# Attention and two feed-forward layers on one core: remaining queries' scores as 64x64 products, and the work around them moved between steps

## The chip, the cores and the metric

One core of one Trainium2 chip runs the kernel. The metric is device time in microseconds (us); lower is better. Three runs of the kernel before gave a median of 1094.99 us (1094.66 to 1095.34).

## The reference

Inputs are float32. Attention has 4 batches of 8 heads, 576 positions, 64 wide; each feed-forward layer (FFN) takes 2304 tokens of 512 through 2048 hidden values.

```python
q_rot, k_rot = (rotate(q), rotate(k))
scores = scale * np.matmul(q_rot, k_rot.transpose(0, 1, 3, 2))
scores = scores - np.max(scores, axis=-1, keepdims=True)
attn = np.exp(scores)
attn = attn / (np.sum(attn, axis=-1, keepdims=True) + 1e-09)
x = np.matmul(attn, v)                                # attention
h = x @ w_in;  x = (h - np.tanh(h)) @ w_out           # first FFN
h = x @ w_in;  x = (h * (1.0 / (1.0 + np.exp(-h)))) @ w_out   # second FFN, other weights
```

## The kernel before

Attention (`attention`, L336) goes through 16 pairs of heads, `i` = 0 to 15. The 576 positions of a head are 4 blocks of 128 (`NJ` = 4, `MAIN` = 512) and 64 remaining ones (`REM`). A pair has nine score tiles: for each of the four query blocks one tile for head 0 and one for head 1 (128 queries by 576 keys), and a ninth with the remaining 64 queries of both heads.

A pair is worked off in five **steps**, `z` = 0 to 4. Steps 0 to 3 each compute the two score tiles of one query block, step 4 the ninth tile. A step issues, in this order:

- `scores` (L501) on PE into two PSUM buffers `sc` that all tiles share in turn. Head 0 sits in rows 0 to 63 of the array and head 1 in rows 64 to 127; each tile is two products of 288 keys. A float32 product shows as two records in the trace, so a step has eight. The ninth tile multiplies all 128 rows by a block-diagonal copy `qr` of the remaining queries (L510).
- transposes on PE: `qk_turn` (L428) turns rotated q and k of the **next** pair into `kq`, one half of the partitions at a time (for halves 0 and 1 in the steps that `QK_K` = (4, 0) names; for pair 0 `QK_0`); `p_turn` (L564) turns the previous step's probabilities `p` with 64x64 transposes for the two halves of partitions in turn; `full_block` (L700) has 128x128 transposes: `rest_turn` (L592, the last 128 columns of two `p` tiles, in steps 3 and 4), `spread` (L541, the reciprocal sums) and `rem_turn` (L440, remaining positions of the next pair).
- `row_max` (L515) on DVE, `exps` (L520) on ACT, and copies of the transposes out of PSUM. `early` copies come before the exponentials on ACT, `outs` after them. `ON_DVE` names the (`u`, half) copies of `p_turn(u)` that DVE does; ACT does the others.
- one or more small pieces (`conv.run`, L753) of the conversion of FFN weights, on DVE and ACT.
- `pv` (L600) on PE: 20 products of `v` with the previous pair's turned probabilities, `PV_N` = (6, 4, 6, 4, 0) of them per step. They run in twos, one for each half of the output partitions of one PSUM tile `x`.

The rotations of pair `i + 2` run on POOL. Transposes go into three PSUM buffers `tp` in turn, `p` has three SBUF buffers. Each engine takes its instructions in the order written here; nothing else sets it. In the last pair (`i` = 15) `on_scores_near` (L1188) splits the first FFN block `xin` into a high part `xh` (ACT) and a low part `xl` (DVE), and after step 4 the first FFN product (`gemm_h`, L814) starts. In pair 0 the stretches without work on PE have dummy transposes (`warm`, L484).

```python
            if h < 2:
                r, c0 = half[h], REM - h * REM
                l = kq[r, 1, REM + j * 128:REM + (j + 1) * 128]
            else:
                r, c0, l = slice(0, 128), REM, qr2[i % 2]
            if i == NP - 1 and z:
                on_scores_near(z)
```

Of the kernel before, what the change touches and what calls it, by code (L numbers as in the profile page):

```python
# [8 lines left out]
F32 = mybir.dt.float32  # L9
# [4 lines left out]
ACTF = mybir.ActivationFunctionType  # L14
# [15 lines left out]
def kernel(  # L30
# [14 lines left out]
    B, H, S, D = q.shape  # L45
# [5 lines left out]
    NJ = S // 128  # L51
# [274 lines left out]
    NPV = 4 * (NJ + 1)  # L326
    Q0 = 256
    WARM = (5, 5, 6, 2, 4, 1, 6)
    WARM_Z = (0, 7, 7, 5, 3)
    ON_DVE = ((1, 1), (2, 1), (4, 0), (4, 1))  # L330
    QK_K, QK_0 = (4, 0), (4, 3)
    R_K = 1
    PV_N = (6, 4, 6, 4, 0)
    CONV_K = (0, 1, 1, 1, 1)

    def attention(conv, on_rope_done, on_scores_near, on_scores_done):  # L336
# [10 lines left out]
        csq = rp.tile([128, 2, NJ, D], F32, name="csq")  # L347
        csr = rp.tile([128, 2, D], F32, name="csr")
        vr2 = [ap.tile([128, 2, D], F32, name=f"vr{i}") for i in range(2)]
        qr2 = [qkp[i].tile([128, 128], F32, name=f"qr{i}") for i in range(2)]  # L350
        raw_t, rot_t, v_t, qk_t = {}, {}, {}, {}
        half = (slice(0, 64), slice(64, 128))

# [87 lines left out]
            PE.transpose(tp, rot_t[i][2].rearrange("p h d -> p (h d)"), ident)  # L441

        def rem_evict(i, tp):
            for r in half:
                ACT.activation(out=qr2[i % 2][r, r], in_=tp[r, 0:64], func=ACTF.Copy)
            ACT.activation(out=qk_t[i][:, 0].rearrange("p (a c) -> p a c", c=REM)[:, ::S // REM],
                           in_=tp[:, 64:128].unsqueeze(1).to_broadcast([128, 2, REM]), func=ACTF.Copy)

# [10 lines left out]
        def q_rope(j0, j1):  # L459
            xm, xr = raw_t[0]  # L460
            if j0 == 0:
                rot_t[0][1] = rp.tile([128, NJ, 2, D], F32, tag="aq", name="aq", bufs=2)
            js = slice(j0, j1)
            sh = [128, 2, j1 - j0, D]
            o = rot_t[0][1][:, js].rearrange("p j h d -> p h j d")
            x = xm[1].rearrange("p h (j d) -> p h j d", j=NJ)[:, :, js]
            b = ap.tile([128, 2, S], F32, tag="p", name="p", bufs=3)[:, :, 0:(j1 - j0) * D]
            b = b.rearrange("p h (j d) -> p h j d", d=D)
            hd = D // 2
            DVE.tensor_tensor(out=o, in0=x, in1=csq[:, 0, js].unsqueeze(1).to_broadcast(sh), op=ALU.mult)  # L470
# [30 lines left out]
        def scores(g):  # L501
            i, n = divmod(g, NTI)
            h, j = tiles[n]
            kq = qk_t[i]
            sc = score_tile(g)
            if h < 2:
                r, c0 = half[h], REM - h * REM
                l = kq[r, 1, REM + j * 128:REM + (j + 1) * 128]
            else:
                r, c0, l = slice(0, 128), REM, qr2[i % 2]  # L510
            for e in range(2):
                PE.matmul(sc[:, e, 0:HALF], lhsT=l, rhs=kq[r, 0, c0 + e * HALF:c0 + (e + 1) * HALF],  # L512
                          start=True, stop=True)
# [6 lines left out]
        def exps(g):  # L520
            i, n = divmod(g, NTI)
            if n == 0:
                sum_t[i] = ap.tile([128, NTI], F32, tag="sums", name="sums", bufs=2)
            sc, st = s_t.pop(g), st_t.pop(g)
            h, u = tiles[n]
            if h != 1:
                p_t[i, u] = ap.tile([128, 2, S], F32, tag="p", name="p", bufs=3)
            p = p_t[i, u][:, h % 2]
            ACT.activation(out=p.rearrange("p (e s) -> p e s", e=2), in_=sc[:, :, 0:HALF],  # L529
                           func=ACTF.Exp, bias=st, accum_out=sum_t[i][:, n:n + 1])  # L530
# [33 lines left out]
        def p_turn(i, u):  # L564
# [10 lines left out]
                cols = [p0 + c * 128 for c in range(NJ) for p0 in (0, S + REM)]  # L575
            else:
                cols = [c * 128 for c in range(NJ)] + [S - 128]
            for x, c in enumerate(cols):
                for w, r in enumerate(half):
                    PE.transpose(tp[w][:, x * 64:x * 64 + 64], p[r, c:c + 128], ident[r, r])  # L580

            def out(w):
                act = (u, w) not in ON_DVE
                if u < NJ:
                    evac(ptm[:, :, :, o + 64 * w:o + 64 * w + 64],
                         tp[w].rearrange("p (c h q) -> p c h q", c=NJ, h=2), act)
                else:
                    evac(ptm[:, :, w, o:o + 64], tp[w][:, 0:MAIN // 2].rearrange("p (c q) -> p c q", c=NJ), act)
                    evac(ptr[half[w], o:o + 64], tp[w][64:128, MAIN // 2:MAIN // 2 + 64], act)
            return [((u, w) not in ON_DVE, lambda w=w: out(w)) for w in range(2)]  # L590

        def rest_turn(i, e, t, act):  # L592
            for a in range(2):
                PE.transpose(t[:, a * 128:a * 128 + 128],  # L594
                             p_t[i, 2 * e + a].rearrange("p h s -> p (h s)")[:, MAIN:MAIN + 128], ident)
            return act, lambda: evac(pt_t[i][e][1][:, 0:Q0], t, act)

        x_t = {}

# [42 lines left out]
        nc.sync.dma_start(out=csk, in_=cs_main)  # L642
        nc.scalar.dma_start(out=csr, in_=cs_rem)
        load_qk(0)
        for t in (*vr2, *qr2):
            DVE.memset(t, 0.0)
        load_v(0)
        load_qk(1)
# [24 lines left out]
        i = z = 0  # L673
        while True:
            live, more = i < NP, i + 1 < NP
            qk_at = QK_K if i else QK_0
            n0 = i * NTI + 2 * z
            gs = range(n0, n0 + (2 if z < NJ else 1)) if live else ()
            if live:
# [20 lines left out]
            def full_block():  # L700
                if live:
                    es = ((), (1,), (), (0,), ())[z] if i else ()
                else:
                    es = (1, 0) if z == 1 else ()
                rest = live and z in (3, NJ)
                rem = more and z == (R_K if i else 3)
                if rest or rem or es:
                    tp = ps.tile([128, 512], F32, tag="tp", name="tpb", bufs=3)
                if rest:
                    (early if z == NJ else outs).append(rest_turn(i, z - 3, tp[:, Q0:], z == NJ))  # L710
# [31 lines left out]
            if live:  # L742
                for _ in range(4):
                    if rq:
                        rq.pop(0)[1]()
            for g in gs:
                exps(g)
            for act, f in outs:
# [515 lines left out]
```

## Time and profile before

| what | value |
|---|---|
| median of three runs | 1094.99 us |
| the profiled execution | 1093.34 us |
| its span, first to last instruction | 1091.6 us |
| PE busy | 1077.0 us (99%) |
| DVE busy | 826.0 us (76%) |
| ACT busy | 647.5 us (59%) |
| POOL busy | 239.2 us (22%) |

A busy PE in this table is a matmul in flight, and matmuls overlap: two half-array matmuls side by side count once, and a half array that waits beside one that works counts as busy. So 99% does not say that PE could not be faster; the start times in the timeline do. DMA moves 126 MB in 91276 packets, 36% of its engines' time.

### The profile page before, as it was taken

Reading aid. Unit: us, or ns where it says so; the run is one execution under the profiler, and the core shown is the slowest. Engines: PE = TensorE matmul, PEld = TensorE weight load, DVE = VectorE, ACT = ScalarE, POOL = GpSimd, SP = SyncE. Lnnn points to the kernel's source line nnn. Section 1 sums busy time; section 2 is a strip of 40 time slices with the busy share of each in tenths; the row PEclk is TensorE's granted clock in tenths of the full one; section 3 lists DMA queues with packets and bytes.
Section 4 is the critical chain, followed back from the end, with each engine's and each line's share of the span. In section 5 each row is a group of like instructions: output and inputs, shape, how many; then the busy total and the mean of one; then the engine's idle time right before and its main releaser. Section 6 shows DMA issues by size and latency. Waiting matters only on the chain.

```text
span 1091.6 us, 18837 instructions
## 1 busy us (share of the span) xinstructions
PE 1077.0 (99%) x6925; PEld 880.8 (81%) x6925; DVE 826.0 (76%) x1425; ACT 647.5 (59%) x1395; POOL 239.2 (22%) x311
## 2 busy tenths in 40 slices
PE   9899999999999999999999999999999999999998
PEld 7676767676678898888888898888888889999997
DVE  6777777777679967988999978987546356767775
ACT  6787877778666766667666666544334335333342
POOL 6776676864010200211001100310000000000000
PEclk9999999999999999999999999999999999999999
DMA  6232323332403530444465541665345112122042
GB/s 177 66 109 82 111 80 111 86 109 60 138 17 126 173 107 20 157 152 146 156 210 174 173 136 48 209 216 183 117 135 183 58 40 97 58 78 87 24 142 77
DMA packets 91276, 126.34 MB, mean 116 GB/s; under 512 B 16432, under 2 KB 57008, under 8 KB 91184
## 3 DMA queue, kind: packets, MB, share of 16 engines
q1 hardware_dynamic: 90592, 124.75, 36.0%
q8 instruction: 54, 0.88, 0.3%
q10 hardware_dynamic: 592, 0.39, 0.1%
q14 instruction: 38, 0.31, 0.1%
HBM read 88.93 MB, written 36.18 MB: 115 GB/s over the span
## 4 chain that ended last, share of the span: by engine, by line
PE 94%; POOL 2%; ACT 2%; DMA 1%; DVE 1%; issue 1%; SPq 0%; POOLq 0%; ACTq 0%; DVEq 0%
PE hp L827 36%; PE acc L904 27%; PE sc L512 9%; PE x L615 8%; PE M L988 7%; PE tpp L580 3%; PE tpq L435 1%; PE acc L1132 1%; PE tpb L545 1%; ACT kq L436 1%; PE tpb L594 1%; POOL bm L417 1%; ACT p L529 0%; DMA xm<-in_k_dram 0%; DMA csr<-rope_rem_dram 0%
## 5 line engine op out<-in xcount | busy, mean ns | idle before, releaser
L827 PE MATMUL hp<-xh,w 128*128 128x512 f32 (+1 forms) x1280 | 389.4, 370 | 0.5 <-ACT xh L808 0.5
L827 PEld LDWEIGHTS hp<-xh,w 128*128 128x128 f32 x1280 | 235.3, 189 | 42.4 <-issue 1.3
L827 PE MATMUL hp<-xl,w 128*128 128x512 f32 (+1 forms) x640 | 236.9, 370 | 0.2 <-DVE xl L809 0.2
L838 ACT ACTIVATE t<-hp 128x512 f32<-128x512 f32 (+1 forms) x120 | 66.8, 556 | 244.0 <-PE hp L827 241.4
L904 PE MATMUL acc<-gh,w 128*128 128x512 f32 (+1 forms) x640 | 193.9, 369 | 0.0
L872 DVE TENSOR_TENSOR gl<-t,gh 128x512 fp32r<-128x512 f32 (+1 forms) x120 | 77.0, 642 | 112.4 <-ACT gh L870 112.2
L517 DVE TENSOR_REDUCE st<-sc 128x1 f32<-128x576 f32 x144 | 104.5, 754 | 63.1 <-PE sc L512 48.4
L827 PEld LDWEIGHTS hp<-xl,w 128*128 128x128 f32 x640 | 121.1, 189 | 19.8 <-DVE xl L809 0.5
L529 ACT ACTIVATE p<-sc,st 128x576 f32<-128x576 f32 x144 | 105.4, 737 | 53.1 <-DVE st L517 45.6
L904 PEld LDWEIGHTS acc<-gh,w 128*128 128x128 f32 x640 | 117.3, 189 | 20.2 <-issue 0.3
L251 POOL TENSOR_TENSOR w<-wf,w 128x512 fp32r<-128x512 f32 x32 | 45.5, 1435 | 349.9 <-ACT w L250 345.1
L904 PE MATMUL acc<-gl,w 128*128 128x512 f32 (+1 forms) x320 | 117.9, 369 | 0.0
L512 PE MATMUL sc<-kq 64*128 64x288 f32 x512 | 100.3, 429 | 2.7 <-ACT p L529 0.6
L512 PEld LDWEIGHTS sc<-kq 64*128 64x128 f32 x512 | 63.3, 186 | 32.5 <-ACT p L529 20.9
L904 PE MATMUL acc<-w,gh 128*128 128x512 f32 x288 | 89.0, 390 | 0.0
L615 PE MATMUL x<-pt,vm 128*64 128x256 f32 (+1 forms) x512 | 75.8, 418 | 0.0
L870 ACT ACTIVATE gh<-t 128x512 fp32r<-128x512 f32 (+1 forms) x120 | 70.6, 588 | 6.2 <-PE acc L904 6.2
L988 PE MATMUL M<-w,gh 128*128 128x256 f32 x384 | 70.3, 283 | 0.0
L904 PEld LDWEIGHTS acc<-gl,w 128*128 128x128 f32 x320 | 60.4, 189 | 10.0
L580 PE MATMUL tpp<-ident,p 64*128 64x64 f32 x1184 | 65.4, 227 | 0.0
L988 PEld LDWEIGHTS M<-w,gh 128*128 128x128 f32 x384 | 61.9, 192 | 2.3
L580 PEld LDWEIGHTS tpp<-ident,p 64*128 64x128 f32 x1184 | 57.7, 140 | 7.4 <-ACT pt L557 2.9
(138 smaller groups left out, 1918.8 us busy)
## 6 DMA issues: line engine op xcount, KB each, us to landing
raw<-in_moe_w_in_dram SPq DMA_DIRECT2D x32, 512.0 KB, 4.1
raw<-in_moe_w_out_dram SPq DMA_DIRECT2D x28, 512.0 KB, 3.8
xin<-xd SPq DMA_DIRECT2D x56, 256.0 KB, 4.6
wd<-wa SPq DMA_DIRECT2D x48, 256.0 KB, 2.2
wf<-wd SPq DMA_DIRECT2D x48, 256.0 KB, 3.9
pd<-xo SPq DMA_DIRECT2D x34, 256.0 KB, 2.8
xo<-pd SPq DMA_DIRECT2D x18, 256.0 KB, 5.2
xm<-in_q_dram SPq DMA_DIRECT2D x16, 256.0 KB, 3.2
```

Source lines behind the costliest of these rows:

```text
L251: (DVE if key[0] == 3 else POOL).tensor_tensor(out=w[:, 1].rearrange("p (a b) -> p a b", a=a), in0=src, in1=w[:, 0].bitcast(F32).rearrange ...
L512: PE.matmul(sc[:, e, 0:HALF], lhsT=l, rhs=kq[r, 0, c0 + e * HALF:c0 + (e + 1) * HALF], start=True, stop=True)
L517: DVE.tensor_reduce(out=st, in_=s_t[g][:, :, 0:HALF], op=ALU.max, axis=AX.XY, negate=True)
L529: ACT.activation(out=p.rearrange("p (e s) -> p e s", e=2), in_=sc[:, :, 0:HALF], func=ACTF.Exp, bias=st, accum_out=sum_t[i][:, n:n + 1])
L580: PE.transpose(tp[w][:, x * 64:x * 64 + 64], p[r, c:c + 128], ident[r, r])
L615: PE.matmul(x[o, 0:w], lhsT=l, rhs=r, start=(cc == 0), stop=(cc == NJ))
L827: PE.matmul(hp, lhsT=w[:, a, ws], rhs=bb, start=(n == 0), stop=(n == 3 * KD - 1))
L838: ACT.activation(out=t, in_=hp, func=ACTF.Tanh, scale=0.5 if l else 1.0)
L870: ACT.activation(out=gh, in_=t, func=ACTF.Copy)
L872: DVE.tensor_tensor(out=gl, in0=t, in1=gh.bitcast(F32), op=ALU.subtract)
L904: PE.matmul(acc, lhsT=a, rhs=bb, start=(fi == 0 and n == 0), stop=(fi == NH - 1 and n == 2))
L988: PE.matmul(prod_t[name][:, tt], lhsT=al[i], rhs=bw[j], start=(first and tt == 0 and x == 0), stop=(last and tt == nt - 1 and x == 2))
```

## The change

- The ninth tile's scores become, for each of two key halves, two products of 64 queries by 288 keys: head 0 in rows 0 to 63 and partitions 0 to 63 of the output, head 1 in rows 64 to 127 and partitions 64 to 127. The remaining queries go into free columns of `kq`; `qr`, its two copies per pair and its two memsets are gone.
- `rest_turn` of step 4 goes. Those columns are turned by `p_turn` of the ninth tile in step 0 of the next pair, as four more 64-row transposes; each half copies its part (`out`). So two `p` tiles live longer, and `p` has four buffers.
- The first half of the ninth tile's copies goes from DVE to ACT (`ON_DVE`).
- `pv` gives 4, 4, 6, 4, 2 products in steps 0 to 4.
- In pair 1 the second `qk_turn` goes from step 0 to step 1 (`QK_AT`), and step 0 gets five dummy transposes (`WARM_Z`).
- In the last pair, steps 2 to 4 have no pieces of weight conversion, and the splits of `xin` go from steps 2, 3 and 4 (one, two, one) to steps 3 and 4 (two each), ahead of the exponentials.

```diff
-    WARM_Z = (0, 7, 7, 5, 3)
-    ON_DVE = ((1, 1), (2, 1), (4, 0), (4, 1))
-    QK_K, QK_0 = (4, 0), (4, 3)
+    WARM_Z = (0, 7, 7, 5, 3, 5)
+    ON_DVE = ((1, 1), (2, 1), (4, 1))
+    QK_AT = ((4, 3), (4, 1), (4, 0))
-    PV_N = (6, 4, 6, 4, 0)
+    PV_N = (4, 4, 6, 4, 2)
...
-            for r in half:
-                ACT.activation(out=qr2[i % 2][r, r], in_=tp[r, 0:64], func=ACTF.Copy)
+            ACT.activation(out=qk_t[i][:, 1, 0:REM], in_=tp[:, 0:64], func=ACTF.Copy)
...
-            if h < 2:
-                r, c0 = half[h], REM - h * REM
-                l = kq[r, 1, REM + j * 128:REM + (j + 1) * 128]
-            else:
-                r, c0, l = slice(0, 128), REM, qr2[i % 2]
             for e in range(2):
-                PE.matmul(sc[:, e, 0:HALF], lhsT=l, rhs=kq[r, 0, c0 + e * HALF:c0 + (e + 1) * HALF],
-                          start=True, stop=True)
+                for w in ((h,) if h < 2 else (0, 1)):
+                    r = half[w]
+                    o, c, n = (slice(0, 128), REM + j * 128, 128) if h < 2 else (r, 0, REM)
+                    k0 = (0 if h == 1 else REM) + e * HALF
+                    PE.matmul(sc[o, e, 0:HALF], lhsT=kq[r, 1, c:c + n], rhs=kq[r, 0, k0:k0 + HALF],
+                              start=True, stop=True)
...
-                p_t[i, u] = ap.tile([128, 2, S], F32, tag="p", name="p", bufs=3)
+                p_t[i, u] = ap.tile([128, 2, S], F32, tag="p", name="p", bufs=4)
...
+            src = [(p, c) for c in cols]
+            if u == NJ:
+                src += [(p_t[i, n].rearrange("p h s -> p (h s)"), MAIN) for n in (NJ - 2, NJ - 1)]
...
+                    evac(ptr[:, 0:Q0].rearrange("p (a b q) -> p a b q", a=2, b=2)[:, :, w],
+                         tp[w][:, MAIN // 2 + 64:MAIN // 2 + 192].rearrange("p (a q) -> p a q", a=2), act)
...
-                rest = live and z in (3, NJ)
+                rest = live and z == 3
...
+            if i == NP - 1 and z >= NJ - 1:
+                on_scores_near(z)
             for g in gs:
                 exps(g)
...
-            conv.run(CONV_K[z] if live else 0)
+            conv.run(CONV_K[z] if i < NP - (z > 1) else 0)
...
-            if i == NP - 1 and z:
-                on_scores_near(z)
...
-        for c in ((), (), (0,), (1, 2), (3,))[z]:
+        for c in (2 * (z - NJ + 1), 2 * (z - NJ + 1) + 1):
             split(0, c)
```

PE, from the ninth tile of a pair (step 4) through step 0 of the next, in a row before:

```order
L512 MATMUL sc<-kq,qr_173 128x288 x2
L594 MATMUL tpb<-ident,p 128x128 x2
L435 MATMUL tpq<-ident,ak 128x64 x4
L435 MATMUL tpq<-ident,aq 128x64 x4
L580 MATMUL tpp<-ident,p 128x64 x16
L512 MATMUL sc<-kq 128x288 x4
L435 MATMUL tpq<-ident,ak 128x64 x4
L435 MATMUL tpq<-ident,aq 128x64 x4
L580 MATMUL tpp<-ident,p 128x64 x10
L615 MATMUL x<-pt_930,vm 64x256 x4
L615 MATMUL x<-pr_931,vr_170 64x256 x2
```

And with the change:

```order
L509 MATMUL sc<-kq 64x288 x4
L434 MATMUL tpq<-ident,ak 128x64 x4
L434 MATMUL tpq<-ident,aq 128x64 x4
L580 MATMUL tpp<-ident,p 128x64 x16
L617 MATMUL x<-pt_936,vm 64x256 x2
L509 MATMUL sc<-kq 128x288 x4
L434 MATMUL tpq<-ident,ak 128x64 x4
L434 MATMUL tpq<-ident,aq 128x64 x4
L580 MATMUL tpp<-ident,p 128x64 x14
L617 MATMUL x<-pt_936,vm 64x256 x2
L617 MATMUL x<-pr_937,vr_170 64x256 x2
```

The two full-array transposes `tpb<-ident,p` are gone from step 4, four half-array ones are added to step 0, and two of v's products (`x`) stand ahead of the next pair's scores.

DVE in the last pair, from the maxima of step 2 to the maximum of the ninth tile (`st<-sc` the row maxima, `xl` the split's low part, `wa` the weight conversion), before:

```order
L517 TENSOR_REDUCE st<-sc 128x1 x2
L559 COPY pt_4609<-tpp 128x8x64
L144 SCALAR_TENSOR_TENSOR wa<-raw,wa 128x512
L624 TENSOR_TENSOR xs<-x,rs 128x320
L809 TENSOR_TENSOR xl_4702<-xin,xh_4701 128x512
L517 TENSOR_REDUCE st<-sc 128x1 x2
L559 COPY pt_4711<-tpp 128x8x64
L559 COPY pr_4610<-tpb 128x256
L148 SCALAR_TENSOR_TENSOR wa<-raw,wa 128x512
L809 TENSOR_TENSOR xl_4756<-xin,xh_4755 128x512
L809 TENSOR_TENSOR xl_4760<-xin,xh_4759 128x512
L517 TENSOR_REDUCE st<-sc 128x1
```

And with the change:

```order
L514 TENSOR_REDUCE st<-sc 128x1 x2
L556 COPY pt_4654<-tpp 128x8x64
L626 TENSOR_TENSOR xs<-x,rs 128x320
L514 TENSOR_REDUCE st<-sc 128x1 x2
L556 COPY pt_4747<-tpp 128x8x64
L556 COPY pr_4655<-tpb 128x256
L811 TENSOR_TENSOR xl_4779<-xin,xh_4778 128x512
L811 TENSOR_TENSOR xl_4783<-xin,xh_4782 128x512
L514 TENSOR_REDUCE st<-sc 128x1
```

No split stands ahead of the maxima of step 3 any more, and the conversion's pieces are gone from here.

## Rows read from the trace of the kernel before

**Rows 1.** Windows: stretch, us; busy us (instructions) of PE, PEld, DVE, ACT, POOL; clock; DMA

```profile
45.00:274.60 229.60, 227.79 (x2288) 161.20 (x2288) 176.88 (x313) 180.22 (x469) 154.45 (x220) 1.00 0.33 94
...
310.00:500.00 190.00, 190.00 (x938) 160.41 (x937) 159.72 (x267) 130.09 (x254) 17.70 (x12) 1.00 0.34 111
```

**Rows 2.** Windows of steps 1, 2 and 3 of pair 11

```profile
208.10:211.59 3.49, 3.49 (x39) 2.29 (x37) 2.57 (x6) 1.40 (x5) 2.92 (x5) 1.00 0.37 108
211.59:215.25 3.66, 3.66 (x38) 2.30 (x36) 2.32 (x4) 3.60 (x13) 3.58 (x6) 1.00 0.06 16
215.25:218.85 3.60, 3.60 (x38) 2.71 (x37) 3.30 (x7) 3.10 (x8) 3.44 (x6) 1.00 0.20 57
```

**Rows 3.** Timeline of PE, step 4 of pair 10 to step 1 of 11: start, duration, work

```profile
201.19 1.24 PE L512 MATMUL sc<-kq,qr 128*128 128x288 f32 x4
202.26 0.38 PE L594 MATMUL tpb<-ident,p 128*128 128x128 f32 x2
202.57 0.46 PE L435 MATMUL tpq<-ident,ak 64*128 64x64 f32 x4
...
203.12 0.71 PE L580 MATMUL tpp<-ident,p 64*128 64x64 f32 x16
203.97 1.96 PE L512 MATMUL sc<-kq 64*128 64x288 f32 x8
...
206.66 1.08 PE L615 MATMUL x<-pt,vm 128*64 128x256 f32 x8
...
208.10 1.25 PE L512 MATMUL sc<-kq 64*128 64x288 f32 x8
```

**Rows 4.** Timeline of ACT over the same stretch

```profile
203.32 0.60 ACT L436 ACTIVATE kq<-tpq 128x512 f32<-128x512 f32 x1 [0.25 <-PE tpq L435]
203.81 0.73 ACT L529 ACTIVATE p<-sc,st 128x576 f32<-128x576 f32 x1
...
206.09 0.74 ACT L529 ACTIVATE p<-sc,st 128x576 f32<-128x576 f32 x1 [0.48 <-DVE st L517]
...
207.55 0.59 ACT L436 ACTIVATE kq<-tpq 128x512 f32<-128x512 f32 x1
210.23 0.74 ACT L529 ACTIVATE p<-sc,st 128x576 f32<-128x576 f32 x1 [2.09 <-DVE st L517]
```

**Rows 5.** Waits of pairs 2 to 14: who for whom, us in total, times, longest

```profile
PEld sc L512 <- ACT p L529: 22.8, 52, 0.5
```

**Rows 6.** Timeline of ACT, step 2 of pair 11

```profile
212.62 0.40 ACT L549 ACTIVATE rs<-tpb 128x256 f32<-128x256 f32 x1
212.89 0.45 ACT L552 ACTIVATE rs<-tpb 64x64 f32<-64x64 f32 x2
213.36 0.45 ACT L445 ACTIVATE qr<-tpb 64x64 f32<-64x64 f32 x2
213.82 0.28 ACT L446 ACTIVATE kq<-tpb 128x128 f32<-128x128 f32 x1
213.99 0.73 ACT L529 ACTIVATE p<-sc,st 128x576 f32<-128x576 f32 x1
```

**Rows 7.** Timeline of PE in pair 1

```profile
29.65 0.27 PE L435 MATMUL tpq<-ident,aq 64*128 64x64 f32 x1 [1.63 <-POOL aq L421]
...
33.01 0.55 PE L545 MATMUL tpb<-ident,rw 128*128 128x128 f32 x3 [1.07 <-POOL rw L537]
```

**Rows 8.** Timeline of DVE, step 3 of the last pair

```profile
287.52 1.35 DVE L809 TENSOR_TENSOR xl<-xin,xh 128x512 fp32r<-128x512 f32 x1 [1.43 <-ACT xh L808]
288.79 1.41 DVE L517 TENSOR_REDUCE st<-sc 128x1 f32<-128x576 f32 x2
```

**Rows 9.** Timeline of PE behind it

```profile
290.52 1.24 PE L512 MATMUL sc<-kq,qr 128*128 128x288 f32 x4 [1.74 <-ACT p L529]
...
296.93 0.49 PE L827 MATMUL hp<-xh,w 128*128 128x512 f32 x1 [0.46 <-ACT xh L808]
```

**Rows 10.** Window behind that wait, columns as in rows 1

```profile
292.00:295.40 3.40, 3.40 (x22) 2.80 (x23) 2.56 (x4) 2.10 (x6) 0.00 (x0) 0.50 0.73 214
```

More of the change, by code (lines that the diff above doesn't have):

```diff
@@ L349, in attention @@
         vr2 = [ap.tile([128, 2, D], F32, name=f"vr{i}") for i in range(2)]
-        qr2 = [qkp[i].tile([128, 128], F32, name=f"qr{i}") for i in range(2)]
         raw_t, rot_t, v_t, qk_t = {}, {}, {}, {}
@@ L466, in q_rope @@
             x = xm[1].rearrange("p h (j d) -> p h j d", j=NJ)[:, :, js]
-            b = ap.tile([128, 2, S], F32, tag="p", name="p", bufs=3)[:, :, 0:(j1 - j0) * D]
+            b = ap.tile([128, 2, S], F32, tag="p", name="p", bufs=4)[:, :, 0:(j1 - j0) * D]
             b = b.rearrange("p h (j d) -> p h j d", d=D)
@@ L577, in p_turn @@
                 cols = [c * 128 for c in range(NJ)] + [S - 128]
-            for x, c in enumerate(cols):
+            src = [(p, c) for c in cols]
+            if u == NJ:
+                src += [(p_t[i, n].rearrange("p h s -> p (h s)"), MAIN) for n in (NJ - 2, NJ - 1)]
+            for x, (t, c) in enumerate(src):
                 for w, r in enumerate(half):
-                    PE.transpose(tp[w][:, x * 64:x * 64 + 64], p[r, c:c + 128], ident[r, r])
+                    PE.transpose(tp[w][:, x * 64:x * 64 + 64], t[r, c:c + 128], ident[r, r])
             def out(w):
@@ L589, in out, with rest_turn @@
                     evac(ptr[half[w], o:o + 64], tp[w][64:128, MAIN // 2:MAIN // 2 + 64], act)
+                    evac(ptr[:, 0:Q0].rearrange("p (a b q) -> p a b q", a=2, b=2)[:, :, w],
+                         tp[w][:, MAIN // 2 + 64:MAIN // 2 + 192].rearrange("p (a q) -> p a q", a=2), act)
             return [((u, w) not in ON_DVE, lambda w=w: out(w)) for w in range(2)]
-        def rest_turn(i, e, t, act):
+        def rest_turn(i, t):
             for a in range(2):
                 PE.transpose(t[:, a * 128:a * 128 + 128],
-                             p_t[i, 2 * e + a].rearrange("p h s -> p (h s)")[:, MAIN:MAIN + 128], ident)
-            return act, lambda: evac(pt_t[i][e][1][:, 0:Q0], t, act)
+                             p_t[i, a].rearrange("p h s -> p (h s)")[:, MAIN:MAIN + 128], ident)
+            return False, lambda: evac(pt_t[i][0][1], t, False)
         x_t = {}
@@ L644, in attention @@
         load_qk(0)
-        for t in (*vr2, *qr2):
+        for t in vr2:
             DVE.memset(t, 0.0)
@@ L675, in attention @@
             live, more = i < NP, i + 1 < NP
-            qk_at = QK_K if i else QK_0
+            qk_at = QK_AT[min(i, 2)]
             n0 = i * NTI + 2 * z
@@ L709, in full_block @@
                 if rest:
-                    (early if z == NJ else outs).append(rest_turn(i, z - 3, tp[:, Q0:], z == NJ))
+                    outs.append(rest_turn(i, tp[:, Q0:]))
                 for e in es:
@@ L752, in attention @@
                 pvq.extend((i - 1, m) for m in range(NPV))
-            conv.run(CONV_K[z] if live else 0)
-            if not i:
-                warm(WARM_Z[z], idle)
+            conv.run(CONV_K[z] if i < NP - (z > 1) else 0)
+            if i * (NJ + 1) + z < len(WARM_Z):
+                warm(WARM_Z[i * (NJ + 1) + z], idle)
             for _ in range(PV_N[z] if live or z == 0 else NPV // 2):
```

## The prediction

> **What bounds the kernel now.** First the windows [rows 1]: from 310 us on PE has no idle microsecond, so what the change does to the FFN layers can cost only if weights come late. In attention PE also counts as busy for 227.79 of 229.60 us, but there a half array that waits beside a working one counts as busy, so I went on to the timeline of PE [rows 3], whose start times show what it waits for, and to ACT over the same stretch [rows 4]. One pair takes 17.66 us (229.60 / 13); its steps 0 to 4 take 4.13, 3.49, 3.66, 3.60 and 2.78 us [rows 2, 3].
>
> The reader should see one thing in rows 3: the same eight score records last 1.96 us in step 0 and 1.25 us in step 1. In step 0 head 1's half starts 0.71 us after head 0's. Its PSUM buffer is that of the ninth tile, whose exponential ends at 204.54 [rows 4]; 203.97 + 0.71 = 204.68, so a release takes 0.14 us. That exponential stands on ACT behind the copy `kq`, which waits for the transposes of step 4; head 0 itself waits for that copy (it ends at 203.92). This kind of wait, weight load behind exponential, occurs 52 times in 13 pairs, four per pair [rows 5].
>
> From this comes a second bound, a **loop** through PE, DVE and ACT. Step 1's scores start at 208.10 and its first exponential at 210.23, 2.13 later [rows 3, 4]; two exponentials take 1.46 (206.09 to 207.55) [rows 4]; with the release, head 1 of a step can't start before 2.13 + 1.46 + 0.14 = 3.73 us after the step before it started. Step 1 takes 3.49 us, so step 2 has a stagger of 0.24, and it costs that. Step 2 takes 3.66, so step 3 would have 0.07; but its exponentials start 0.27 late (213.99, where 211.59 + 2.13 = 213.72), behind copies on ACT [rows 6], so 0.34.
>
> **Steady pairs, step by step.**
>
> *Ninth tile's scores.* Now four full-array records, 1.07 us (201.19 to 202.26) [rows 3]. New: eight records on a quarter of the array each, two at a time if the diagonal quarters run side by side. Then it is 1.07 again; one after the other it is 2.14. I take 1.07: the two heads' half-height products run side by side in step 1 (eight in 1.25), and v's products, two halves of the columns into one tile `x`, run side by side too: twelve records in 1.44 (206.66 to 208.10), 0.24 for two [rows 3]. The Trainium skill, TensorEngine Tiling, section "Gotcha 1: PSUM Pressure", says that different row tiles cannot use the same PSUM bank at once, and the two heads' products here go to one bank. No run here shows it; by the rows the sum below comes out at 1085.5, by that rule at rival (a)'s time.
>
> *Step 4 loses two 128x128 transposes.* They take 0.31 (202.26 to 202.57) [rows 3], of which I take 0.22, since some of it is the change of array shape behind full-array work, which stays. Bounds 0.2 and 0.31. The `kq` copy and the ninth exponential wait for the transposes behind them and come 0.22 earlier; the ACT copy of what these two made goes too.
>
> *Two of v's products move from step 0 to step 4.* Step 0 loses 0.46. Step 4 gains 0.46 and a change of shape in and out, for which I take 0.2, between nothing and 0.4. PE's own work in step 4 is now 2.48: eight half-array transposes take 0.55 (202.57 to 203.12), so the sixteen that run two by two end at about 203.67 [rows 3], and 0.30 is waiting. New: 2.48 - 0.22 + 0.66 = 2.92. So the products stand in a hole, and `kq` (0.05 + 203.92 - 0.22, or 2.56 after the step's start) no longer holds anything. The ninth buffer is free at 3.49 - 0.22 = 3.27, a stagger of 0.35 in place of 0.71.
>
> *Step 0.* 4.13 - 0.71 is 3.42; less 0.46 for v; plus 0.14 for two more side-by-side transposes per half (0.07 each). 3.10, and 0.35 of stagger: 3.45. Steps 4 and 0 together 6.37, now 6.91: **0.54 gained**.
>
> *Step 1 gives some back.* The loop now asks for 3.73 - 3.45 = 0.28 of stagger, where step 0 was long enough before. And the copies of the first half of the ninth tile, now on ACT, stand behind `kq`: second exponential at 2.86 from step 0's start, `kq` at 3.59, the first copy 0.49 later (as 203.32 to 203.81) [rows 4], then copies of 256, 64 and 128 columns at 0.27, 0.235 and 0.28 [rows 6]: done at 4.87, 4.97 with the signal. Step 1's second half of transposes wants that `tp` buffer at 3.45 + 0.28 + 1.07 = 4.80. I take 0.15, between nothing and 0.3. Step 1: 3.49 + 0.28 + 0.15 = 3.92.
>
> *Steps 2 and 3.* Step 1 now fills the loop: step 2 loses its stagger, 3.42. Step 3 gets 3.73 - 3.42 = 0.31 of stagger on 3.26 of own work, 3.57; that the remaining queries take one copy instead of two 0.23 ones [rows 6] removes ACT's delay there.
>
> Sum: 2.92 + 3.45 + 3.92 + 3.42 + 3.57 = 17.28, **0.38 less per pair**, 13 pairs (2 to 14): **4.9 us**. What is late next is the loop itself: in steps 0 to 3 the exponentials, not PE, then set the pace.
>
> **Pair 1.** Its step 0 waits 1.63 us for POOL's rotation of q, and step 1 another 1.07 for the reciprocals, which are behind both [rows 7]. With the second `qk_turn` in step 1, the first wait falls into work; POOL's end (29.65) does not move, so the reciprocals come only some 0.4 us earlier, and the five dummies and the loop fill part. Of 2.7 us I take 1.1, between 0.5 and 2.
>
> **Last pair.** DVE's split `xl` stands ahead of step 3's maxima; it waits 1.43 us for ACT and runs 1.35 [rows 8]. So the ninth tile starts after 1.74 us of idle PE [rows 9]. The split now comes behind the maxima and this wait goes; I take 1.55, a stagger of step 3 staying. Behind the wait the clock is granted at 0.50 (1.2 instead of 2.4 GHz) for 3.4 us [rows 10]. At the other level the same work would take at most 1.7 us less, and less than that where PE waited for a copy. PE does not idle ahead of it any more, so I count 1.4. The wait for the last `xh` (0.46) [rows 9] goes too, since its split is issued ahead of the ninth exponential: 0.5 with what hangs on it. Step 0 of this pair is bound by the loop and gains nothing. Together **3.5 us**.
>
> **At nothing:** the fourth `p` buffer (needed, since step 0 reads two `p` tiles of the pair before; no wait on `p` shows now); DVE's shorter list in step 0; the memsets at the start; the three pieces of weight conversion that come later, hidden as long as PE has no gap in the FFN [rows 1]. On SP's queue one weight load moves behind the loads of `xin`, which helps these. The bound on this group is 1 us of loss.
>
> **Sum.** 4.9 + 1.1 + 3.5 = 9.5 us from the profiled execution's 1093.34 (span 1091.6): 1083.8. The median of the runs is 1.65 higher, so 1094.99 - 9.5 = **1085.5 us**.
>
> **Rivals.** (a) *The diagonal quarters take turns.* Both write one PSUM bank, and no row of this kernel shows two halves of the rows doing that: the heads in step 1 write different tiles, v's halves write one tile but use all rows. Then step 4 takes 1.07 us more in each of 16 pairs, `kq` and the ninth exponential shift by as much, and nothing absorbs it: 17.1 - 9.5 = 7.6 us slower, 1102.6. It decides from 0.6 us per pair on. Against it: v's halves in one tile show that two halves of the partitions can be written at once [rows 3]. Chance 0.12.
>
> (b) *The loop eats the steady gain.* If the stagger of step 1 and ACT's copies (0.28 + 0.15; with the copies at their upper bound 0.58) take back what steps 4 and 0 give, only the ends are left: 1094.99 - 4.6 = 1090.4. For it: three of five steps already run at the loop's pace. Against it: step 2 gets its 0.24 back. Chance 0.2.
>
> (c) *More than I count.* A stagger need not cost its whole length, because transposes of the other half can fill it; without the cost of ACT's copies and half the staggers it is about 0.7 per pair, 4.2 us more: 1081.3. Chance 0.13. The forecast has the remaining 0.55.
>
> **How the numbers follow.** About 0.2% (2.2 us) is what a measurement here can tell from no change. Forecast, (b) and (c) hold 0.88 and are all faster by more; I take 0.07 off for (b) with the ends worth half, which lands within (0.06) or beyond (0.01); (a) is slower by more. Faster 0.81, same 0.06, slower 0.13. The range from 1080.5 to 1090.5 takes in the bounds of the terms and (b) and (c), and leaves out (a).
>
> **What would show it.** Right: the ninth tile's eight records end within about 1.3 us; step 0's score row shrinks from 1.96 to about 1.6 us; pairs come every 17.3 us; no stretch at 0.50 between 285 and 300 us, no 1.74 us wait there, and none of 1.63 in pair 1. Wrong: the ninth tile's records take over 2 us (a); step 1 grows beyond 4 us with its transposes waiting for ACT's copies (b); a PE gap after 310 us.

## The result and the profile after

The changed kernel has a median of 1085.74 us (four runs, 1085.18 to 1085.87). The kernel before, run four times, has 1094.90 us (the first three of these runs gave the 1094.99 that the forecast starts from). The ratio is 0.9915, with a 95% interval from 0.9898 to 0.9932: **faster by 0.85%**. The profiled execution of the changed kernel takes 1085.18 us with a span of 1083.4 us, against 1093.34 and 1091.6 before.

The first part of the page of the changed kernel, with busy time, share and instructions of each engine:

```profile
PE 1071.4 (99%) x7026; PEld 874.3 (81%) x7026; DVE 817.6 (75%) x1407; ACT 650.1 (60%) x1411; POOL 240.1 (22%) x311
```

It tells little, like the one before. The times at which the two traces reach the same point tell more. All are in us from the start of the span, read from the starts of PE's records:

| point | before | after | gained by then | gained in this stretch |
|---|---|---|---|---|
| first scores of pair 2 | 45.01 | 43.68 | 1.33 | 1.33 |
| first scores of pair 15 | 274.61 | 265.12 | 9.49 | 8.16 (pairs 2 to 14) |
| ninth tile of pair 15 | 290.52 | 279.20 | 11.32 | 1.83 |
| first FFN product | 293.04 | 281.55 | 11.49 | 0.17 |
| fifth block of FFN products | 315.70 | 301.32 | 14.38 | 2.89 |
| 52nd block of FFN products | 551.08 | 536.70 | 14.38 | 0 |
| 53rd block of FFN products | 556.52 | 548.35 | 8.17 | **-6.21** |
| end of the span | 1091.6 | 1083.4 | 8.2 | 0 |

So attention and the entry to the FFN gave 14.4 us, more than forecast, and one place in the FFN took 6.2 back. (The blocks are counted from the first FFN product on, 12 records `hp` each.)

**A steady pair.** Windows of the changed kernel: step 4 of pair 10 and steps 0 to 3 of pair 11, then three stretches that come up below (columns as in [rows 1]):

```profile
194.15:196.99 2.84, 2.84 (x39) 1.74 (x37) 2.31 (x4) 1.82 (x5) 2.76 (x4) 1.00 0.82 214
196.99:200.50 3.51, 3.51 (x41) 2.64 (x39) 2.78 (x7) 2.71 (x8) 0.02 (x1) 1.00 0.46 146
200.50:204.19 3.69, 3.69 (x39) 2.58 (x37) 2.40 (x7) 3.00 (x11) 3.16 (x6) 1.00 0.39 115
204.19:207.64 3.45, 3.45 (x38) 2.29 (x36) 2.11 (x4) 3.24 (x10) 3.37 (x5) 1.00 0.03 5
207.64:211.18 3.54, 3.54 (x38) 2.71 (x36) 3.24 (x6) 3.29 (x10) 3.38 (x6) 1.00 0.25 62
544.50:547.90 3.40, 3.40 (x9) 2.66 (x10) 2.59 (x5) 0.00 (x0) 0.00 (x0) 0.50 0.41 103
270.00:290.00 20.00, 19.67 (x173) 13.05 (x172) 13.26 (x26) 15.37 (x37) 1.30 (x2) 1.00 0.45 142
285.00:300.00 15.00, 14.67 (x90) 9.31 (x86) 9.73 (x19) 9.00 (x20) 1.30 (x2) 1.00 0.07 23
```

A pair takes 17.03 us instead of 17.66. The forecast was 17.28, and of its steps only step 1 is far off: 3.69 instead of 3.92.

The timeline of PE over the same steps answers to [rows 3]:

```profile
194.15 1.19 PE L509 MATMUL sc<-kq 64*64 64x288 f32 x8
195.27 0.46 PE L434 MATMUL tpq<-ident,ak 64*128 64x64 f32 x4
195.57 0.28 PE L434 MATMUL tpq<-ident,aq 64*128 64x64 f32 x2
195.64 0.27 PE L580 MATMUL tpp<-ident,p 64*128 64x64 f32 x1
195.69 0.22 PE L434 MATMUL tpq<-ident,aq 64*128 64x64 f32 x1
...
196.41 0.65 PE L617 MATMUL x<-pt,vm 128*64 128x256 f32 x4
196.99 1.64 PE L509 MATMUL sc<-kq 64*128 64x288 f32 x8
```

The eight quarter-size records leave PE after 1.12 us (194.15 to 195.27): they run two by two. Step 0's scores last 1.64 us (1.96 before), a stagger of 0.40.

**The end of attention.** DVE of the changed kernel in steps 3 and 4 of the last pair, against [rows 8]:

```profile
276.92 1.42 DVE L514 TENSOR_REDUCE st<-sc 128x1 f32<-128x576 f32 x2 [0.58 <-PE sc L509]
278.25 0.68 DVE L556 COPY pt<-tpp 128x512 f32<-128x512 f32 x1
278.85 0.42 DVE L556 COPY pr<-tpb 128x256 f32<-128x256 f32 x1
279.18 1.29 DVE L811 TENSOR_TENSOR xl<-xin,xh 128x512 fp32r<-128x512 f32 x2
280.44 0.76 DVE L514 TENSOR_REDUCE st<-sc 128x1 f32<-128x576 f32 x1
```

The maxima of step 3 wait for the scores alone, the splits come behind them, and neither wait of [rows 9] has a counterpart. The ninth tile starts at 279.20 here, so the place to compare with [rows 10] lies before 290 us. From 270 to 300 us the clock is granted at 1.00 (last two of the windows above), where [rows 10] had 0.50.

**A new wait in the FFN.** The timeline of PE of the changed kernel from 530 us on:

```profile
539.19 0.39 PE L829 MATMUL hp<-xh,w 128*128 128x512 f32 x1
543.01 0.50 PE L906 MATMUL acc<-gh,w 128*128 128x512 f32 x1 [3.43 <-ACT w L250]
543.34 0.40 PE L906 MATMUL acc<-gl,w 128*128 128x512 f32 x1
544.36 1.12 PE L906 MATMUL acc<-gh,w 128*128 128x512 f32 x2 [0.62 <-POOL w L251]
```

Behind the two waits (4.05 us together) the clock is at 0.50 for 3.4 us (the window from 544.50). PE waits for a weight `w` that ACT (L250) and POOL (L251) split into a high and a low part. ACT's timeline shows the order it stands in:

```profile
541.11 0.72 ACT L853 ACTIVATE s<-u,sqa 128x512 f32<-128x512 f32 x1
541.72 0.72 ACT L854 ACTIVATE mk<-u,ht 128x512 bf16<-128x512 f32 x1
542.33 0.62 ACT L250 ACTIVATE w<-wf 128x512 fp32r<-128x512 f32 x1
```

This split comes at 542.33, behind ACT's work on the block before. In the trace of before the same split, the sixteenth at L250, starts at 535.52, 18.3 us before the first product that uses its weight (553.80). In the change its data does not explain this: the loads `wf` are issued on SP by 515.8 us, 26 us ahead of the split. What is late is the place of the split in the program.

### The profile page after: what moved, and what is told of

It is laid out like the page before. It is cut to its first block, busy times and chain, and to the rows that moved or that the text cites. A ratio compares the mean times of both kernels' runs of the same rounds, so it can differ in the third digit from the quotient of the medians.

```text
span 1083.4 us, 19054 instructions
## 1 busy us (share of the span) xinstructions
PE 1071.4 (99%) x7026; PEld 874.3 (81%) x7026; DVE 817.6 (75%) x1407; ACT 650.1 (60%) x1411; POOL 240.1 (22%) x311
## 4 chain that ended last, share of the span: by engine, by line
PE 94%; issue 2%; POOL 2%; ACT 1%; DMA 1%; DVE 0%; SPq 0%; POOLq 0%; DVEq 0%
PE hp L829 35%; PE acc L906 26%; PE sc L509 9%; PE x L617 8%; PE M L990 7%; PE tpp L580 4%; PE tpq L434 1%; PE acc L1134 1%; PE tpb L542 1%; PE tpb L596 1%; DMA wf<-wd 0%; POOL bm L416 0%; ACT p L526 0%; DMA xm<-in_k_dram 0%; POOL w L251 0%
## 5 line engine op out<-in xcount | busy, mean ns | idle before, releaser
L251 POOL TENSOR_TENSOR w<-wf,w 128x512 fp32r<-128x512 f32 x32 | 45.4, 1431 | 355.8 <-ACT w L250 352.3
L509 PE MATMUL sc<-kq 64*128 64x288 f32 (+1 forms) x640 | 115.0, 426 | 0.8 <-ACT p L526 0.6
L509 PEld LDWEIGHTS sc<-kq 64*128 64x128 f32 (+1 forms) x640 | 68.9, 175 | 41.3 <-ACT p L526 16.1
L617 PE MATMUL x<-pt,vm 128*64 128x256 f32 (+1 forms) x512 | 79.1, 421 | 0.0
L580 PE MATMUL tpp<-ident,p 64*128 64x64 f32 x1248 | 68.2, 225 | 0.0
L580 PEld LDWEIGHTS tpp<-ident,p 64*128 64x128 f32 x1248 | 63.5, 138 | 4.0 <-DVE xl L811 0.4
```

Source lines behind the costliest of these rows:

```text
L251: (DVE if key[0] == 3 else POOL).tensor_tensor(out=w[:, 1].rearrange("p (a b) -> p a b", a=a), in0=src, in1=w[:, 0].bitcast(F32).rearrange ...
L509: PE.matmul(sc[o, e, 0:HALF], lhsT=kq[r, 1, c:c + n], rhs=kq[r, 0, k0:k0 + HALF], start=True, stop=True)
L580: PE.transpose(tp[w][:, x * 64:x * 64 + 64], t[r, c:c + 128], ident[r, r])
L617: PE.matmul(x[o, 0:w], lhsT=l, rhs=r, start=(cc == 0), stop=(cc == NJ))
```

## The experiments

The steady step times in this section are medians over pairs 2 to 14 of the starts of the score records. Most experiments have one execution, and the start of a run differs by some tenths of a microsecond, so for terms of a few tenths these starts count and not the total time. The kernel before took 1093.05 us (median of 7) beside e1 to e4, 1094.30 (one run) beside e5 to e8, and 1094.26 (one run) beside e9 and e10.

### Where do the 6.2 us in the FFN come from?

The theory: the three weight-conversion pieces that the last pair no longer does come later in the FFN, so one converted weight is finished one block later, and with it the loads of the 32nd weight. Its split is made in the program by `fetch.fill`, which in this pass may be called in each block only until `m < 5 * NH + NH`. One block later the rule has ended, and the split waits until the product that needs it asks for it. The rival: the work moved in attention makes a transfer late, and the pieces have no part in it.

**e1**, the changed kernel with the pieces back:

```diff
-            conv.run(CONV_K[z] if i < NP - (z > 1) else 0)
+            conv.run(CONV_K[z] if live else 0)
```

> The changed kernel, with the last pair's three pieces of weight conversion (steps 2 to 4) as they were. The changed kernel has a PE wait of 3.43 us and one of 0.62 us at 543 us and 3.4 us at half clock behind it, 6.2 us in all between tick 51 and tick 52 of the FFN. Theory 1, the pieces: three pieces later means that the last weight of the second pass is split in tick 51 and not 47, so PE waits; with them back the wait and the half clock go, and the last pair loses at most 1 us to them: 1079.5 us (1079.0 to 1080.5). Theory 2, the early start: the FFN starts 14.4 us earlier, and the weight's transfer does not keep up; then the wait stays, 1085.5 to 1086.5.

Measured: 1079.18 us (median of 4), ratio 0.9872 (0.9857 to 0.9887), an interval apart from the change's. The 52nd block takes 5.44 us as before, without a wait (the window below, columns as in [rows 1]), and ACT makes the split at 521.62:

```profile
515.63 0.63 ACT L250 ACTIVATE w<-wf 128x512 fp32r<-128x512 f32 x1
521.62 0.62 ACT L250 ACTIVATE w<-wf 128x512 fp32r<-128x512 f32 x1
...
537.19:542.63 5.44, 5.44 (x26) 4.50 (x24) 4.18 (x8) 3.35 (x7) 0.00 (x0) 1.00 0.42 123
```

SP issues the loads `wf` for it at 508.36, in the change at 514.15, about one block later. The period of a pair stays 17.03, and the last pair does without its waits too. So leaving the pieces out of the last pair costs 6.2 us and gives 0.2 back (36.20 us from the start of pair 15 to the fifth FFN block in the change, 36.38 in e1). **This version is faster than both kernels.**

**e2**, the changed kernel, pieces late as in it, with the rule two blocks longer:

```diff
-                fetch.fill((2, int(f % NH > 3 or m < 5 * NH + NH), 3)[p])
+                fetch.fill((2, int(f % NH > 3 or m < 5 * NH + NH + 2), 3)[p])
```

> The changed kernel; only the rule for when the FFN issues the next weight split goes on for two ticks more (until tick 49, now until tick 47), so the late split is issued in tick 48. The pieces stay late. Theory 1, the pieces and this rule together: the wait at 543 us goes, 1079.5 us (1079.0 to 1080.0), and the last pair keeps what it has. Theory 2, the early start: the transfer of the weight lands at the same place as now and PE still waits 2 us or more: 1083 to 1086.

Measured: 1080.18 us, ratio 0.9883 (0.9866 to 0.9899). That is 0.2 above the range that I had expected. The wait and the half clock are gone, the 52nd block takes 5.44. The split stands at 526.94, later than in e1 and early enough. So it is the rule of the program and not the conversion's speed that made the weight late.

**e3**, the kernel before with the pieces taken from the last pair as in the change:

```diff
-            conv.run(CONV_K[z] if live else 0)
+            conv.run(CONV_K[z] if i < NP - (z > 1) else 0)
```

> The kernel before, with nothing of the change but the last pair's three pieces left out of steps 2 to 4 (they come later). Theory 1: the same wait of some 4 us and the half clock appear near 557 us although nothing starts earlier: 6.2 us slower, less 0 to 1 us that the last pair gains: 1100 to 1101. Theory 2: no wait, 1094 to 1095.

Measured: 1097.87 us, 4.8 slower than before on that chip. PE's timeline of e3 at two places:

```profile
295.26 0.49 PE L827 MATMUL hp<-xh,w 128*128 128x512 f32 x1 [1.95 <-ACT xh L808]
...
555.72 0.50 PE L904 MATMUL acc<-gh,w 128*128 128x512 f32 x1 [3.43 <-ACT w L250]
556.06 0.40 PE L904 MATMUL acc<-gl,w 128*128 128x512 f32 x1
557.08 1.06 PE L904 MATMUL acc<-gh,w 128*128 128x512 f32 x2 [0.62 <-POOL w L251]
```

The waits of 3.43 and 0.62 are the same to the hundredth in a kernel that has nothing else of the change, and the 53rd block begins 11.64 us after the 52nd. That rules the rival out. I had expected 1100 to 1101, which is 5 to 6 us above before, because I did not see how much fewer pieces help the last pair: step 3 falls from 5.12 to 3.37, and the wait of 1.74 [rows 9] is gone although the splits stand where they did. Then the wait for `xh` grows from 0.46 to 1.95, and of this gain 1.7 us are left at the fifth block.

### The steady pair, part by part

**e4**, e1 with v's products as before:

```diff
-    PV_N = (4, 4, 6, 4, 2)
+    PV_N = (6, 4, 6, 4, 0)
```

> As e1, with v's products back at 6, 4, 6, 4, 0 per step. Against e1's period of about 17.04 us per pair. Theory, the hole: step 4 then waits for kq again (2.5 us instead of 2.84), step 0 has a stagger of 0.7 and two more products (4.25 instead of 3.51), step 1 loses its stagger (3.49), step 2 gets one (3.68), step 3 loses most of it (3.3): 17.2 us, and 2.5 us more in all than e1. Rival: moving the products only costs two changes of the array's shape; then the period is 16.8 to 16.9 and the kernel 2 us faster than e1.

**e5**, e1 with the first half of the ninth tile's copies back on DVE:

```diff
-    ON_DVE = ((1, 1), (2, 1), (4, 1))
+    ON_DVE = ((1, 1), (2, 1), (4, 0), (4, 1))
```

> As e1, with the first half of the ninth tile's copies back on DVE. Against e1's period of 17.03 us. Theory of the prediction: on ACT these copies hold up step 1's transposes by 0.15 us; back on DVE step 1 shrinks from 3.69 to 3.55, and the kernel gains 2 us. Theory from the trace after: step 1's transposes wait for DVE's copies, not for ACT's, and those end early enough; but DVE's list in step 0 gets 0.87 us longer, so that step 1's maxima, which start 1.27 us after its scores, come some 0.3 us later, and with them the release of the score buffers: step 2 grows by 0.2 to 0.3, 3 to 4 us more than e1.

**e6**, e1 with the block-diagonal copy of the remaining queries again:

```diff
-            ACT.activation(out=qk_t[i][:, 1, 0:REM], in_=tp[:, 0:64], func=ACTF.Copy)
+            for r in half:
+                ACT.activation(out=qr2[i % 2][r, r], in_=tp[r, 0:64], func=ACTF.Copy)
...
+            if h == 2:
+                for e in range(2):
+                    PE.matmul(sc[:, e, 0:HALF], lhsT=qr2[i % 2], rhs=kq[:, 0, REM + e * HALF:REM + (e + 1) * HALF],
+                              start=True, stop=True)
+                return
```

> As e1, with the ninth tile's scores as two products with the block-diagonal copy of the queries, as before (two copies on ACT again, 0.23 us each, instead of one). Theory of the prediction: the products themselves took 1.07 us either way, only ACT's second copy counts, and it stands behind step 1's exponentials with some 0.18 us of room: step 3 at most 0.1 us longer, 17.03 to 17.13 us per pair, 0 to 1.5 us more than e1. Rival: the quarters of the array save PE something of their own (loads of smaller weights, or no change to the full shape); then step 4 grows by 0.2 us or more, 3 us or more in all.

**e7**, e5 with the 128x128 transposes in step 4 again, and without the four half-array ones in step 0:

```diff
-            if u == NJ:
-                src += [(p_t[i, n].rearrange("p h s -> p (h s)"), MAIN) for n in (NJ - 2, NJ - 1)]
...
-                rest = live and z == 3
+                rest = live and z in (3, NJ)
```

> As e1, with the last columns of the probabilities turned in step 4 by two full-array transposes and copied by ACT ahead of kq, as before, and the ninth tile's copies all on DVE, as before. Theory of the prediction: step 4 grows by 0.22 to 0.31 us and kq, the ninth exponential and the stagger of step 0 come as much later; step 0 loses 0.14: 17.2 to 17.3 us per pair, 2 to 3.5 us more than e1. Rival: the transposes fill time in which PE waits anyway; then the period stays within 0.05.

**e10**, the kernel before with nothing but v's products moved:

```diff
-    PV_N = (6, 4, 6, 4, 0)
+    PV_N = (4, 4, 6, 4, 2)
```

> The kernel before with v's products at 4, 4, 6, 4, 2 per step and nothing else. By the sum of the prediction: step 4 takes 2.48 + 0.58 = 3.06 us, the ninth buffer is free at 3.49, stagger 0.43; step 0 takes 4.13 - 0.71 - 0.42 + 0.43 = 3.43; step 1 has a stagger of 0.3 and takes 3.79; step 2 loses its own, 3.42; step 3 takes 3.57: 17.27 us per pair instead of 17.66, 5 us less in all than before. Rival: the gain needs the other two parts (nothing in step 4 ahead of kq), and alone this gives less than 0.2 us per pair.

Measured, the five steps and their sum, us:

| kernel | 0 | 1 | 2 | 3 | 4 | pair | time of the run |
|---|---|---|---|---|---|---|---|
| before | 4.13 | 3.49 | 3.67 | 3.60 | 2.78 | 17.66 | |
| e10: before, v moved | 3.33 | 3.87 | 3.46 | 3.60 | 3.15 | 17.41 | 1090.29 |
| e7: also 64x64 products | 3.33 | 3.87 | 3.45 | 3.54 | 3.25 | 17.45 | 1085.95 |
| e5: also turned by halves | 3.50 | 3.87 | 3.48 | 3.52 | 2.84 | 17.21 | 1082.90 |
| e1: also copies on ACT | 3.51 | 3.69 | 3.46 | 3.54 | 2.83 | 17.03 | 1079.18 |
| the change | 3.51 | 3.70 | 3.46 | 3.54 | 2.84 | 17.03 | 1085.74 |
| e4: e1, v as before | 4.26 | 3.49 | 3.67 | 3.33 | 2.51 | 17.26 | 1080.98 |
| e6: e1, block diagonal | 3.50 | 3.70 | 3.45 | 3.60 | 2.89 | 17.14 | 1080.39 |

From before down to e1 the parts come one by one (e7 to e1 also have the change's ends, which the pair does not show). Four things follow.

*The hole in step 4 is there.* v's two products make step 4 0.37 (e10) or 0.32 us (e4 against e1) longer and step 0 0.80 or 0.75 shorter. Step 1 gets 0.38 or 0.20 longer, step 2 0.21 shorter in both, and step 3 is 0.21 longer in e1 than in e4. What remains is 0.25 and 0.23 us per pair, so the rival of e4 (moving them only costs) and that of e10 (less than 0.2) both fall. In e10 the run is 4.0 us faster, 1 less than expected, and the period is 17.41 and not 17.27: steps 4 and 1 are 0.09 and 0.08 longer than I had worked out, step 0 is 0.10 shorter. e4 is 1.8 us above e1, where I had expected 2.5.

*Turning by halves is worth 0.24 us per pair* (e7 to e5): step 4 loses 0.41, step 0 gains 0.17. The two transposes themselves take 0.37 of it in e7 (199.22 to 199.59; 0.31 before). e7 is a miss of mine: I had expected 17.2 to 17.3 us per pair and at most 3.5 us over e1, and it came at 17.45 and 6.8 over. Of the 0.42 per pair, 0.18 is the copies on DVE (e5 to e1, below).

*The 64x64 products alone are worth nothing until then.* With the 128x128 transposes behind them (e10 to e7), step 4 gets 0.10 longer and step 3 0.06 shorter. Once those are gone (e6 against e1), they are worth 0.11: 0.06 in step 3, where I had expected it from ACT's second copy, and 0.05 in step 4, where I had expected none. The rival, 0.2 us or more in step 4, falls.

*The copies on ACT are a gain of 0.18 us per pair, all in step 1* (e5 to e1), where the prediction had counted a loss of 0.15. In the waits of e5 from 44 to 265 us (who for whom, total, times, longest) stands a line that e1 has no counterpart of; there PE never waits for `rw` in this stretch:

```profile
PEld tpb L542 <- POOL rw L534: 3.1, 13, 0.2
```

In e5 the copy stands on DVE ahead of the reciprocal of the sums, which POOL then spreads (`rw`) for PE. POOL starts at 203.78 there, after waiting 3.48 us for that reciprocal, and PE waits 0.2 us for POOL in each of 13 pairs. In e1 POOL starts 0.45 us after step 1's first scores (201.25 to 200.80), in e5 1.33 (203.78 to 202.45). So the change took this copy out of a chain of DVE, POOL and PE that the prediction did not look at ("DVE's shorter list in step 0" stood under nothing). I had expected the cost of e5 in step 2; it is in step 1, and the run as a whole is 3.7 us above e1 as expected. The maxima of step 1 do come later, 1.47 us after its scores (e1 1.27). By the loop of the prediction that delay alone would have put about as much into step 2, so taking POOL's wait away by itself need not give the 0.18; no run separates the two.

And the loss that I had counted does not occur. ACT of the changed kernel, against [rows 4]:

```profile
196.01 0.60 ACT L435 ACTIVATE kq<-tpq 128x512 f32<-128x512 f32 x1 [1.01 <-PE tpq L434]
196.51 0.74 ACT L526 ACTIVATE p<-sc,st 128x576 f32<-128x576 f32 x1
...
200.56 0.60 ACT L435 ACTIVATE kq<-tpq 128x512 f32<-128x512 f32 x1
201.03 0.39 ACT L554 ACTIVATE pt<-tpp 128x256 f32<-128x256 f32 x1
201.45 0.51 ACT L554 ACTIVATE pr<-tpp 64x64 f32<-64x64 f32 x2
```

The copies end at 201.96, 4.97 after step 0's start, as late as I had worked out. But PE goes on in step 1 all the while:

```profile
200.50 1.46 PE L509 MATMUL sc<-kq 64*128 64x288 f32 x8
201.57 0.88 PE L580 MATMUL tpp<-ident,p 64*128 64x64 f32 x16
202.38 0.55 PE L542 MATMUL tpb<-ident,rw 128*128 128x128 f32 x3
```

All sixteen transposes lie between 201.57 and 202.45, and nine of them have started by 201.96. A half has eight, so the second half did not wait for the end of ACT's copies. The likely reason is that it goes into the buffer that DVE's copies freed (199.60 to 200.56), and only `spread` (202.38) into the one that ACT copied last, so that I had assigned the three `tp` buffers wrongly; the profile does not show which buffer an instruction writes.

### The ends of attention

**e8**, e1 with pair 1 as before:

```diff
-    WARM_Z = (0, 7, 7, 5, 3, 5)
+    WARM_Z = (0, 7, 7, 5, 3)
...
-    QK_AT = ((4, 3), (4, 1), (4, 0))
+    QK_AT = ((4, 3), (4, 0), (4, 0))
```

> As e1, with pair 1's second turn of q and k back in step 0 and without the five dummy transposes. Theory: PE waits 1.6 us for POOL's rotation of q again, and from the start of pair 1 to the start of pair 2 it takes 18.4 to 18.9 us instead of 17.86: 0.5 to 1 us more than e1. Rival: POOL's end sets the start of pair 2 either way, no difference over 0.2 us.

Measured: 1079.60 us. Pair 2 starts at 44.12 us (e1 44.00, the change 43.68, before 45.01). So 0.9 of the 1.3 us gained by then does not need this part. What the part is worth does not stand out from the starts: the change, e1, e2 and e9, which are the same up to here, reach pair 2 between 43.68 and 44.26. From the start of pair 1 to that of pair 2, the measure that I had named, e8 takes 17.45 us (from 26.67), less than e1 with 17.86, and not 18.4 to 18.9. So my theory failed; the rival (POOL's end sets the start of pair 2 either way) fits better, with 0.12 us between the starts of pair 2 in e8 and e1. PE's wait for POOL's q in e8 is 0.81 us, half of the 1.63 of [rows 7]. Moving the transposes removed PE's wait for POOL's q in step 0 and left the one in step 1, `spread` for POOL's `rw`: that wait ends at 32.04 in the change (0.80 of waiting, with step 0 begun 1.4 us earlier than in e8), at 32.48 in e8 (0.28) and at 33.01 before (1.07, [rows 7]).

**e9**, e1 with the splits of `xin` in their places before:

```diff
-            if i == NP - 1 and z >= NJ - 1:
-                on_scores_near(z)
...
+            if i == NP - 1 and z:
+                on_scores_near(z)
...
-        for c in (2 * (z - NJ + 1), 2 * (z - NJ + 1) + 1):
+        for c in ((), (), (0,), (1, 2), (3,))[z]:
```

> As e1, with the splits of the FFN's first block back in steps 2, 3 and 4 of the last pair, behind the exponentials. Theory: a split's DVE half stands ahead of step 3's maxima again and waits for ACT, which has the pieces of weight conversion ahead of its own half: step 3 of the last pair takes 4.8 to 5.2 us instead of 3.63, PE idles over 1.5 us, the clock falls to half behind that, and the kernel takes 3.5 to 4.5 us more than e1. Rival: with the pieces and without the old order of the last pair the wait is something else's, and the kernel stays within 1 us of e1.

Measured: 1083.74 us, span 1081.9, 4.3 more than e1's 1077.6. Step 3 of the last pair takes 5.30 us (e1 3.63). From the start of pair 15 to the fifth FFN block it is 40.42 us (e1 36.38, the change 36.20, before 41.09). PE's timeline of e9 there:

```profile
281.53 1.19 PE L509 MATMUL sc<-kq 64*64 64x288 f32 x8 [1.68 <-ACT p L526]
...
287.89 0.49 PE L829 MATMUL hp<-xh,w 128*128 128x512 f32 x1 [1.59 <-ACT xh L810]
```

And two windows of e9, from the ninth tile to the first FFN product and from there to the second block:

```profile
281.53:283.96 2.43, 2.43 (x28) 1.33 (x28) 1.72 (x4) 2.43 (x6) 0.00 (x0) 1.00 0.02 3
283.96:290.88 6.92, 5.09 (x36) 3.10 (x35) 3.19 (x6) 3.83 (x9) 0.00 (x0) 1.00 0.69 226
```

With the pieces in the last pair, the places of the splits alone are worth 4 us. The clock stays at 1.00 here after a wait of 1.68, against my expectation, and still the first FFN block takes 6.92 us (7.19 before, with the half clock; 4.54 in the change): the wait for the last `xh` takes the place of the slow stretch, 1.59 instead of 0.46. That split stands on ACT behind the ninth exponential and its copies in both.

Four kernels have the splits in their old places. From the ninth tile to the fifth FFN block they take 25.19 us (before) and 25.14 (e10) with the half clock, 25.18 (e3) and 24.58 (e9) without; with the new places it is 22.12 (the change) and 22.22 (e1). So what the half clock of [rows 10] cost does not show in the time; PE would have waited for `xh` anyway.

## Why the prediction came out right, and where it was wrong

1085.5 was forecast and 1085.74 measured, but that the figure is so close is luck. By the traces attention and the entry to the FFN gave 4.9 us more than forecast, one place in the FFN took 6.2 that were counted at nothing, and about 1 us more comes from which executions were profiled (below). Of the signs that the prediction named, the right ones came (but pairs every 17.03 us and not 17.3), and so did a wrong one: "a PE gap after 310 us".

*Steps 4 and 0:* right. 0.54 us gained were forecast, 0.56 measured (2.78 + 4.13 against 2.84 + 3.51). The diagonal quarters run side by side, so rival (a) falls: the ninth tile takes 1.12 us and not 2.14, though both heads write one bank. The Trainium skill's rule that different row tiles cannot access one bank at once (TensorEngine Tiling (Array Packing), "Gotcha 1: PSUM Pressure") is not borne out for this pair of tiles, whose outputs lie in different partitions.

*Step 1:* "I take 0.15, between nothing and 0.3" failed; its lower end was true. The loop's own share was right: 3.73 - 3.51 = 0.22 of stagger, and the step is 0.21 longer than before. Steps 2 and 3 were forecast at 3.42 and 3.57 and came at 3.46 and 3.54. Step 4 is 0.08 shorter than forecast; that transposes of `p` begin there while those of q still run (195.64 and 195.69 in PE's timeline above) may be a part of it. So 4.9 us for pairs 2 to 14 was sized 3.3 too low; it is near rival (c), for one of the reasons given there, the missing cost of ACT's copies. Rival (b) did not occur.

*Pair 1:* 1.1 forecast, 1.33 measured, but by e8 not, as far as can be told, through the part that I put it down to. What gave it is open.

*Last pair:* 3.5 forecast, 4.89 measured. The wait ahead of the ninth tile went as forecast (step 3 from 5.12 to 3.56, 1.56 against 1.55); by e1 and e3 either of two parts, the splits' places or the pieces, takes it away. The terms for the half clock (1.4) and for `xh` (0.5) were wrong apart: the stretch behind the ninth tile takes the same with and without the half clock, so it was bound by ACT's splits, and the 1.4 is not borne out as a cost of the clock. Together they gave 2.9 (2.65 in the first FFN block, the rest in the next ones) instead of 1.9. Another 0.4 came from steps 0 to 2 of this pair and step 4, counted at nothing.

*"The three pieces of weight conversion that come later, hidden as long as PE has no gap in the FFN"*, with a bound of 1 us: failed, by 6.2. That PE has no idle microsecond before the change [rows 1] shows that no weight is late there, not how far each is from late. And in this program how early a split is made hangs on a rule in blocks, which turns a delay of one block into one of four.

The sum by the trace: 1.3 + 8.2 + 4.9 - 6.2 = 8.2 us instead of 9.5. The medians differ by 9.16, because the profiled execution of before stood 1.56 below its median and that of the change 0.56 below its own.

## What to carry to other kernels

Work that is "moved later, where it is hidden" has to be followed to its last consumer through the rules that place it; a stage without idle time says nothing about the slack of its inputs. Before costing a copy that changes engine, list which buffer it frees, and also who stood behind it on the engine that it leaves: here what stood behind it was worth 0.18 us per pair and the buffer nothing. Where a slow clock and a wait follow each other, ask whether the wait would grow if the slow stretch went.

## What the runs showed of the hardware that was not expected

Two products on diagonal quarters of the array, different rows and different output partitions of one PSUM bank, run side by side: eight records in 1.12 us. Transposes of `p` that stand later in the program start between those of q (195.64, ahead of 195.69); by the program they are those of the other half of the rows. So PE does not always start its instructions in the order written, which the section on the kernel before says of every engine.

The half clock did not follow every wait of the same length near the end of attention. It came after waits of 1.74 us [rows 9] and 1.73 (e10, 0.50 from 287.7 to 291.1 us), and not after 1.68 (e9) or 1.95 (e3). After the 4.05 us in the FFN it came in both kernels that had them, for 3.4 us each time (from 544.5 in the change, from 557.3 in e3). What decides between the first four is open.
